# Symmetric score blocks with DMA-transposed mirrors, and rows scattered by expert, in an attention plus mixture-of-experts kernel

## The chip, the cores and the metric

One core of a Trainium2 chip runs the whole program in one launch. The metric is device time in microseconds (us), the median of three runs. The engines are PE (TensorE matmuls), PEld (TensorE weight loads, which may lie beside matmuls), DVE (VectorE), ACT (ScalarE), POOL (GpSimd) and SP (SyncE, which here only issues transfers). Transfers run on 16 DMA engines, whoever issues them.

## The reference

```python
# attention: u, v are (8, 2816, 256), z is (8, 2816, 64)
scores = (1/2816) * matmul(z, z.transpose(0, 2, 1))   # (8, 2816, 2816)
attn = maximum(scores, 0) ** 2
x = (u * matmul(attn, v)).reshape(22528, 256)
# mixture of experts: 8 experts, hidden size 512
y_dense = maximum(x @ w1_dense, 0) @ w2_dense
logits = x @ w_gate                                   # (22528, 8)
e = argmax(logits);  gate = softmax(logits)[e]
y_moe = gate * (maximum(x @ w1[e], 0) @ w2[e])        # each row uses one expert only
out = y_dense + y_moe
```

Two facts of this arithmetic matter later: `scores` is the product of `z` with itself, so each batch's matrix is symmetric, and each row of `x` needs only the expert that its largest logit names.

## The kernel before

Rows are cut into blocks of 128; a batch has 22 of them. Inputs are float32, matmul operands are cast to bfloat16.

**Attention stage.** For each of 8 batches, `zT` (64 x 2816) is made by 22 TensorE transposes (L59) with a DVE cast each (L61), and `v` is cast by DVE (L68). Six groups of up to four query blocks (512 columns, the last group 256) each run over all 22 key blocks. For a key block, `do_sc` makes a score tile of 128 x 512 (L81), ACT applies relu and the scale (L89), DVE squares it (L90), and two matmuls add its product with `vtile` to `outT` (L100). All 22 x 22 score blocks are computed. `outT` has the features on partitions, so it is copied out, transposed back on TensorE (L113), multiplied by `u` (L121), and written to `x_bridge` in DRAM (L122).

**Weight stage.** All expert weights are loaded in float32 and cast once (L131 to L145).

**Expert stage.** 44 tiles of 512 rows. A tile loads `x_bridge` (L156), transposes it on TensorE, computes logits, and makes a gate row for each expert with two reductions on POOL (L170, L175). The function `ffn` runs for the dense layer and then for every one of the 8 experts, on an input that was multiplied by the gate row of that expert (L208), which is zero for rows that belong elsewhere. All add into `yT`. The result is transposed back and written (L219 to L222). All transfers are issued by SP. A tile scheduler sets the order on each engine.

## Time and profile before

| what | value |
|---|---|
| median of three runs | 2951.72 us (2950.89 to 2952.02) |
| span of the profiled execution, first to last instruction | 2948.5 us |
| mean granted TensorE clock | 0.981 of full speed |
| busy: PE, DVE, ACT, POOL | 2665.0, 1825.7, 1473.0, 221.3 us |
| attention, weight and expert stage in that span | 0 to 1004, 1004 to 1053, 1053 to 2949 us |

The profiled execution has no time of its own beside the span; the median of the runs is 3.2 us longer than the span, and that is taken as what lies around it. Busy time of PE counts each matmul from its start to its end, and neighbours overlap, so 90% of the span is not 90% of what PE can do; the distance from one start to the next tells that. The shares are averages over two long stages with different limits, so the stages are read apart.

### The profile page before, as it was taken

What the parts mean: (1) busy time and instruction counts of PE and PEld (TensorE: products, weight loads), DVE (VectorE), ACT (ScalarE), POOL (GpSimd) and SP (SyncE); (2) the same over time, 40 slices, a digit from 0 to 9 for tenths busy, and PEclk for the clock granted to TensorE, in tenths of its full rate; (3) what the DMA queues carried; (4) which work ended last, traced back from release to release, by engine and by line L of the source; (5) the groups of instructions that cost most, each with busy time, mean ns of one, the idle gap of its engine ahead of it and who ended that gap; (6) DMA issues with size and microseconds to landing.
All of it is one profiled execution on the core that took longest, in us unless ns stands there. A gap on an engine that the chain in (4) does not pass through costs nothing.

```text
span 2948.5 us, 34413 instructions
## 1 busy us (share of the span) xinstructions
PE 2665.0 (90%) x11176; PEld 1020.7 (35%) x11176; DVE 1825.7 (62%) x3586; ACT 1473.0 (50%) x2685; POOL 221.3 (8%) x94
## 2 busy tenths in 40 slices
PE   7999999999999569999999999989899998999997
PEld 2323233232332123333333333333333333333333
DVE  7889888888889645445445544544555455455543
ACT  4556656566566324444444444444444444444443
POOL 0000000000000011011101110110111011101100
PEclk9999999999999879999999999999999999999999
DMA  6231221311111400000000000000000000000000
GB/s 177 88 94 54 93 87 56 94 55 54 40 54 50 159 20 27 30 23 23 28 28 22 24 29 26 22 26 29 24 22 28 29 21 26 27 26 23 26 26 15
DMA packets 165381, 133.18 MB, mean 45 GB/s; under 512 B 45648, under 2 KB 162896, under 8 KB 165200
## 3 DMA queue, kind: packets, MB, share of 16 engines
q1 hardware_dynamic: 165200, 130.99, 14.6%
q8 instruction: 87, 1.43, 0.2%
q14 instruction: 94, 0.77, 0.1%
HBM read 84.42 MB, written 46.14 MB: 44 GB/s over the span
## 4 chain that ended last, share of the span: by engine, by line
PE 60%; DVE 12%; ACT 10%; issue 7%; POOL 7%; DMA 2%; ACTq 0%; DVEq 0%; POOLq 0%; SPq 0%
PE yT L194 19%; PE outT L100 13%; PE h_ps L190 12%; PE sc_ps L81 9%; ACT hs L192 6%; POOL se L175 5%; DVE attn_sb L90 3%; PE scps L204 3%; DVE xTe L208 3%; ACT attn_f L89 3%; POOL mx L170 3%; DVE gw L177 2%; PE tp L113 2%; PE yp L219 2%; PE xp L158 1%
## 5 line engine op out<-in xcount | busy, mean ns | idle before, releaser
L192 ACT ACTIVATE hs<-h_ps 128x512 bf16<-128x512 f32 x1584 | 863.0, 593 | 992.0 <-PE h_ps L190 989.8
L194 PE MATMUL yT<-hs,w2e 128*128 128x512 bf16 x2816 | 796.5, 379 | 117.0 <-ACT hs L192 113.4
L190 PE MATMUL h_ps<-xTe,w1e 128*128 128x512 bf16 x2816 | 800.8, 379 | 0.4 <-DVE xTe L208 0.4
L89 ACT ACTIVATE attn_f<-sc_ps 128x512 f32<-128x512 f32 (+1 forms) x1056 | 585.2, 561 | 411.8 <-DVE attn_sb L90 234.8
L208 DVE TENSOR_TENSOR xTe<-xT,scps 128x512 bf16<-128x512 bf16 x704 | 451.6, 676 | 404.0 <-PE h_ps L190 400.1
L90 DVE TENSOR_TENSOR attn_sb<-attn_f 128x512 bf16<-128x512 f32 (+1 forms) x1056 | 649.2, 639 | 29.0 <-ACT attn_f L89 21.6
L100 PE MATMUL outT<-attn_sb,vtile 128*128 128x512 bf16 (+1 forms) x2112 | 586.1, 370 | 19.0 <-DVE attn_sb L90 13.4
L194 PEld LDWEIGHTS <-w2e 128*128 128x128 bf16 x2816 | 277.4, 101 | 480.9 <-issue 293.5
L190 PEld LDWEIGHTS <-w1e 128*128 128x128 bf16 x2816 | 275.0, 98 | 327.7 <-issue 2.2
L81 PE MATMUL sc_ps<-zT 64*128 64x512 bf16 (+1 forms) x1056 | 367.5, 371 | 17.1 <-ACT attn_f L89 1.8
L170 POOL PARTITION_ALL_REDUCE mx<-lg x44 | 78.4, 1783 | 2582.4 <-DVE lg L167 2582.4
L160 DVE CAST xT<-xp 128x128 bf16<-128x128 f32 x352 | 101.3, 288 | 262.1 <-PE xp L158 261.9
L100 PEld LDWEIGHTS <-vtile 128*128 128x128 bf16 x2112 | 167.6, 103 | 237.3 <-issue 185.2
L177 DVE RECIPROCAL gw<-se 8x512 f32<-8x512 f32 x44 | 147.0, 3342 | 98.6 <-POOL se L175 98.6
L81 PEld LDWEIGHTS <-zT 64*128 64x128 bf16 x1056 | 91.5, 93 | 308.3 <-issue 286.2
L204 PE MATMUL scps<-sca,ones 1*128 1x512 bf16 x352 | 135.2, 384 | 46.1 <-DVE xTe L208 46.1
L221 DVE COPY yo<-yp 128x128 f32<-128x128 f32 x352 | 101.5, 288 | 111.2 <-PE yp L219 65.7
L158 PE MATMUL xp<-ident,xs 128*128 128x128 f32 x352 | 107.6, 306 | 49.8 <-DMA xs<-x_bridge 43.8
L175 POOL PARTITION_ALL_REDUCE se<-ex x44 | 142.2, 3233 | 64.6 <-ACT ex L173 64.6
L117 DVE COPY xt<-tp 128x128 f32<-128x128 f32 x352 | 101.4, 288 | 57.0 <-PE tp L113 54.5
L113 PE MATMUL tp<-ident,oS 128*128 128x128 f32 x352 | 113.3, 322 | 3.9 <-DVE xt L117 1.2
L194 PE MATMUL yT<-hs,w2d 128*128 128x512 bf16 x352 | 109.8, 380 | 4.8 <-ACT hs L192 0.7
(35 smaller groups left out, 985.7 us busy)
## 6 DMA issues: line engine op xcount, KB each, us to landing
vtf<-in_v_dram SPq DMA_DIRECT2D x8, 2816.0 KB, 10.9
ut<-in_u_dram SPq DMA_DIRECT2D x176, 128.0 KB, 2.1
x_bridge<-xt SPq DMA_DIRECT2D x176, 128.0 KB, 1.7
xs<-x_bridge SPq DMA_DIRECT2D x176, 128.0 KB, 2.1
out_dram<-yo SPq DMA_DIRECT2D x176, 128.0 KB, 1.7
c<-in_moe_w_dram SPq DMA_DIRECT2D x2, 4096.0 KB, 20.4
zTf<-in_z_dram SPq DMA_DIRECT2D x8, 704.0 KB, 5.1
sca<-sca_all SPq DMA_DIRECT2D x352, 1.0 KB, 1.6
```

The source lines that it names most:

```text
L81: nc.tensor.matmul(out=sc_ps[k][:], lhsT=zT[:, k * P:(k + 1) * P], rhs=zT[:, i0 * P:i0 * P + W], start=True, stop=True,)
L89: nc.scalar.activation(attn_f[:], sc_ps[k][:], AF.Relu, scale=scale)
L90: nc.vector.tensor_mul(attn_sb[k][:], attn_f[:], attn_f[:])
L100: nc.tensor.matmul(out=outT[d][:], lhsT=vtile[:, k, d * P:(d + 1) * P], rhs=a[:], start=(k == 0), stop=(k == nK - 1),)
L113: nc.tensor.transpose(out=tp[:], in_=oS[d][:, j * P:(j + 1) * P], identity=ident[:],)
L175: nc.gpsimd.partition_all_reduce(se[:], ex[:], E, bass_isa.ReduceOp.add)
L177: nc.vector.reciprocal(gw[:], se[:])
L190: nc.tensor.matmul(out=h_ps[:], lhsT=w1t(fc, d), rhs=xin[d][:], start=(d == 0), stop=(d == 1))
L192: nc.scalar.activation(hs[:], h_ps[:], AF.Relu)
L194: nc.tensor.matmul(out=yT[d][:], lhsT=w2t(fc, d), rhs=hs[:], start=(first and fc == 0), stop=(last and fc == 3))
L204: nc.tensor.matmul(out=scps[:], lhsT=ones1[:], rhs=sca0[:], start=True, stop=True)
L208: nc.vector.tensor_mul(xTe[d][:], xT[d][:], scps[:])
```

## The change

**Attention.** In each batch, `score_chunk` makes only the blocks on and above the diagonal, 253 of 484, in strips: strip `k` holds key block `k` against blocks `k` to 21, in chunks of up to 8 blocks (1024 columns). `end_strip` has SP issue one DMA transpose for a strip, which fills tile `T` with the mirrored blocks. `av` makes one 128-row output block of 256 columns from 22 matmuls; its stationary operand is a block of a strip `A` where `k <= i`, else a block of `T`, so the result already has rows on partitions and no TensorE transpose is left. `zT` and the transposed `x` come from DMA transposes as well (L78, L204). `z` is loaded twice, side by side, so that the contraction is over 128 and the scale is halved. Scores run ahead of `av` by `LEAD` = 9 steps, with 4 buffers for `T`.

**Routing.** Every 11 blocks, `route_a` and `route_b` turn logits into a gate, an expert and a running position within that expert. `scatter` has POOL issue an indirect DMA that writes 128 rows of 576 bytes (x in bfloat16, gate, row number) to their places in DRAM array `xs`. Weights are cast by POOL-issued DRAM-to-DRAM transfers into `wb`.

**Expert stage.** A table made by 32 DVE instructions gives each of 95 tiles of 256 rows (88 and 7 for ragged ends) its start row and its one expert. `fetch` reads both into registers on SP, transposes the rows by DMA, and loads that expert's weights (512 KB) and the gates. A tile runs the dense layer and that one expert; `finish` scales, adds and has POOL scatter the rows to `out`, two indirect DMAs a tile.

The attention core of the new file:

```diff
+        zT = zpool.tile([P, nK, P], BF, name="zT")
+        nc.sync.dma_start_transpose(
+            out=zT[:], in_=zn[:].rearrange("p k h d -> p (k h d)"))
...
+            k0, k1 = h * nK // 2, (h + 1) * nK // 2
+            nc.gpsimd.dma_start(out=vb[:, k0:k1, :], in_=src[:, k0:k1, :])
...
+        def score_chunk(b, k, c0, c1):
+            zT = zT_of[b]
+            w = c1 - c0
+            s_ps = psS.tile([P, 8, P], F32, name="s_ps")
+            for h in range(0, w, 4):
+                hw = min(4, w - h)
+                nc.tensor.matmul(out=s_ps[:, h:h + hw, :], lhsT=zT[:, k, :],
+                                 rhs=zT[:, k + c0 + h:k + c0 + h + hw, :],
+                                 start=True, stop=True)
+            r = aw.tile([P, 8, P], F32, name="r")
+            nc.scalar.activation(r[:, :w, :], s_ps[:, :w, :], AF.Relu, scale=0.5 / S)
+            nc.vector.tensor_mul(A[b, k][:, c0:c1, :], r[:, :w, :], r[:, :w, :])
...
+        def end_strip(b, k):
+            n = nK - 1 - k
+            if n:
+                T[b, k] = aT.tile([P, nK - 1, P], BF, name="T")
+                nc.sync.dma_start_transpose(
+                    out=T[b, k][:, :n, :],
+                    in_=A[b, k][:, 1:, :].rearrange("p n c -> p (n c)"))
...
+        def av(b, i):
+            o = psV.tile([P, D], F32, name="o")
+            vb = v_of[b]
+            for k in range(nK):
+                lhsT = A[b, k][:, i - k, :] if k <= i else T[b, i][:, k - i - 1, :]
+                nc.tensor.matmul(out=o[:], lhsT=lhsT, rhs=vb[:, k, :],
+                                 start=(k == 0), stop=(k == nK - 1))
+            return o
...
+        def gate_x(g, o):
+            pay = pays[(g // G) % 3]
+            x = pay[:, g % G, 0:D]
+            nc.vector.tensor_mul(x, o[:], ut_of.pop(g))
+            xT = aw.tile([P, 2, P], BF, name="xT", bufs=6)
+            nc.sync.dma_start_transpose(out=xT[:], in_=x)
+            xT_of[g] = xT
...
+        def scatter(g):
+            q, j = divmod(g, G)
+            ins = nc.gpsimd.indirect_dma_start(
+                out=xs, out_offset=bass.IndirectOffsetOnAxis(ap=rs[q][:, j:j + 1], axis=0),
+                in_=pays[q % 3][:, j, :].bitcast(F32), in_offset=None)
+            nodep("xs", ins)
...
+        LEAD = 9
+        rate = (nK + 1) / 2
+        for g in range(nB + 8):
+            if g < nB:
+                b, i = divmod(g, nK)
+                must = strip_end[b, min(i + 1, nK - 1)]
+                want = rate * (g + 1 + LEAD * min(1.0, (g + 1) / LEAD) - 1)
+                produce(max(must, want))
```

The expert stage of the new file:

```diff
+        def fetch(s):
+            R = nc.values_load(Rt[0:1, s:s + 1], engines=[ET.SP], min_val=0,
+                               max_val=XROWS - T2,
+                               skip_runtime_bounds_check_because="made by the table")
+            e = nc.values_load(Et[0:1, s:s + 1], engines=[ET.SP], min_val=0, max_val=E - 1,
+                               skip_runtime_bounds_check_because="made by the table")
+            xT = mx.tile([P, 2, T2], BF, name="xT2")
+            rows = xs[bass.ds(R, T2), :]
+            nc.sync.dma_start_transpose(out=xT[:], in_=rows.bitcast(BF)[:, 0:D])
+            we = mx.tile([P, 2 * F + 4 * D], BF, name="we")
+            nc.sync.dma_start(out=we[:], in_=wb[bass.ds(e, 1), :, :].rearrange("o p f -> (o p) f"))
+            me = mx.tile([P, 2, 2], F32, name="me")
+            nc.sync.dma_start(out=me[:], in_=rows[:, P:P + 2]
+                              .rearrange("(j p) c -> p j c", p=P))
+            return xT, we, me
...
+        def up(xT, w1):
+            h_ps = psH.tile([P, 4, T2], F32, name="h_ps")
+            for f in range(4):
+                for c in range(2):
+                    nc.tensor.matmul(out=h_ps[:, f, :], lhsT=w1(c, f), rhs=xT[:, c, :],
+                                     start=(c == 0), stop=(c == 1))
+            h = mh.tile([P, 4, T2], BF, name="h")
+            nc.scalar.activation(h[:], h_ps[:], AF.Relu)
+            return h
...
+        def down(h, w2, name):
+            y = psY.tile([P, 2, D], F32, name=name)
+            for j in range(2):
+                for f in range(4):
+                    nc.tensor.matmul(out=y[:, j, :], lhsT=h[:, f, j * P:(j + 1) * P],
+                                     rhs=w2(f), start=(f == 0), stop=(f == 3))
+            return y
...
+            for j in range(2):
+                nc.vector.tensor_scalar(out=ys[:, j, :], in0=ye[:, j, :], scalar1=me[:, j, 0:1],
+                                        scalar2=None, op0=ALU.mult)
+            nc.vector.tensor_add(ys[:], ys[:], yd[:])
+            for j in range(2):
+                ins = nc.gpsimd.indirect_dma_start(
+                    out=out, out_offset=bass.IndirectOffsetOnAxis(ap=ix[:, j:j + 1], axis=0),
+                    in_=ys[:, j, :], in_offset=None, bounds_check=N - 1, oob_is_err=False)
...
+        AHEAD = 3
+        got = {s: fetch(s) for s in range(AHEAD)}
+        pend = None
+        for s in range(NT + 1):
+            if s < NT:
+                xT, we, me = got.pop(s)
+                hd = up(xT, lambda c, f: w1d[:, c, f * P:(f + 1) * P])
+            if pend is not None:
+                ps_, he_, yd_, we_, me_ = pend
+                ye_ = down(he_, lambda f: we_[:, 2 * F + f * D:2 * F + (f + 1) * D], "ye")
+                finish(ps_, yd_, ye_, me_)
+            if s < NT:
+                if s + AHEAD < NT:
+                    got[s + AHEAD] = fetch(s + AHEAD)
+                he = up(xT, lambda c, f: we[:, c * F + f * P:c * F + (f + 1) * P])
+                yd = down(hd, lambda f: w2d[:, f, :], "yd")
+                pend = (s, he, yd, we, me)
```

**What stands in a row on PE in the attention stage.** Before, in the middle of a group, a score matmul of 512 columns stands between pairs of output matmuls of 512 columns (`sc_ps` the score tile, `outT` the output with features on partitions):

```order
L81 LDWEIGHTS zT
L81 MATMUL sc_ps<-zT 128x512 [waits Activation_49]
L100 LDWEIGHTS vtile
L100 MATMUL outT_4749<-attn_sb,vtile 128x512 [waits DVE_49]
L100 LDWEIGHTS vtile
L100 MATMUL outT_4750<-attn_sb,vtile 128x512
L81 LDWEIGHTS zT
L81 MATMUL sc_ps<-zT 128x512 [waits Activation_49]
```

After, in the middle of a batch, a score chunk comes first and then the 22 output matmuls of a step, 256 columns each, each with its own weights (`A` a strip, `T` a mirrored strip; the first five of the 22 are shown):

```order
L142 MATMUL s_ps<-zT 128x512 [waits Activation_49]
L142 LDWEIGHTS zT
L142 MATMUL s_ps<-zT 128x512
L188 LDWEIGHTS A_4010
L188 MATMUL o<-vb,A_4010 128x256 [waits DVE_49]
L188 LDWEIGHTS A_4077
L188 MATMUL o<-vb,A_4077 128x256
L188 LDWEIGHTS A_4160
L188 MATMUL o<-vb,A_4160 128x256
L188 LDWEIGHTS A_4243
L188 MATMUL o<-vb,A_4243 128x256
L188 LDWEIGHTS T [waits DMAHW2_49]
```

Each output matmul before waited for DVE's square of its own score tile; now the step waits once for DVE to have emptied its output buffer, and at the first block of `T` for a DMA transpose.

**What stands in SP's queue in the attention stage.** Before, plain loads of `u` and `v` and stores of `x`:

```order
L122 DMA x_bridge<-xt 128x256 [waits DVE_49]
L122 DMA x_bridge<-xt 128x256 [waits DMAHW1_49,DVE_49]
L120 DMA ut<-in_u_dram 128x256 [waits DMAHW2_49]
L122 DMA x_bridge<-xt 128x256 [waits DMAHW3_49,DVE_49]
L120 DMA ut<-in_u_dram 128x256 [waits DMAHW4_49]
L120 DMA ut<-in_u_dram 128x256 [waits DMAHW6_49,DMAHW5_49]
L122 DMA x_bridge<-xt 128x256 [waits DVE_49]
```

After, at the end of the second batch's strips, DMA transposes only: `T` is a mirrored strip out of `A14` to `A20`, `xT` the transposed x of one block out of a payload tile:

```order
L204 DMA_TRANSPOSE xT_1799<-pay0_70 128x2x128 [waits DVE_49]
L153 DMA_TRANSPOSE T_1810<-A16_1803 128x5x128 [waits DMAHW2_49,DMAHW3_49,DVE_49,PE_49]
L153 DMA_TRANSPOSE T_1819<-A17_1812 128x4x128 [waits DMAHW5_49,DVE_49,PE_49]
L204 DMA_TRANSPOSE xT_1847<-pay0_70 128x2x128 [waits DMAHW4_49,DVE_49]
L153 DMA_TRANSPOSE T_1857<-A18_1851 128x3x128 [waits DMAHW6_49,DVE_49,PE_49]
L153 DMA_TRANSPOSE T_1865<-A19_1859 128x2x128 [waits DMAHW0_49,DVE_49,PE_49]
L153 DMA_TRANSPOSE T_1873<-A20_1867 128x1x128 [waits DMAHW2_49,DMAHW7_49,DVE_49,PE_49]
L204 DMA_TRANSPOSE xT_1905<-pay0_70 128x2x128 [waits DVE_49]
L204 DMA_TRANSPOSE xT_1963<-pay0_70 128x2x128 [waits DMAHW1_49,DVE_49]
L153 DMA_TRANSPOSE T_1989<-A0_1924 128x21x128 [waits DMAHW3_49,DVE_49,PE_49]
```

The loads moved to POOL's queue. Each `T` waits for PE (a buffer four strips back), and an `xT` that stands behind it waits with it.

**What stands in SP's queue in the expert stage.** Before, a gate row for each expert (`sca`), loads of x and stores of the output:

```order
L156 DMA xs_17762<-x_bridge 128x256 [waits DMAHW7_49,PE_49]
L203 DMA sca0_16926<-sca_all_16641 1x16x32 [waits DMAHW6_49,DMAHW2_49,PE_49]
L203 DMA sca0_17060<-sca_all_17027 1x16x32 [waits DMAHW4_49,DVE_49,PE_49]
L203 DMA sca0_17096<-sca_all_17027 1x16x32 [waits DMAHW6_49,DMAHW0_49,PE_49]
L203 DMA sca0_17132<-sca_all_17027 1x16x32 [waits DMAHW7_49,DMAHW1_49,PE_49]
L156 DMA xs_17376<-x_bridge 128x256 [waits PE_49]
L203 DMA sca0_17168<-sca_all_17027 1x16x32 [waits DMAHW3_49,DMAHW0_49,PE_49]
```

After, one tile's `fetch`: two register loads (TENSOR_LOAD), a DMA transpose, the weights and the gates; the stores moved to POOL:

```order
L418 TENSOR_LOAD Rt_8486
L421 TENSOR_LOAD Et_8487
L425 ISA
L425 DMA_TRANSPOSE xT2_8680<-xs 128x2x256 [waits DMAHW4_49,PE_49]
L427 ISA
L427 DMA we_8682<-wb 128x2048 [waits DMAHW5_49,PE_49]
L429 ISA
L429 DMA me_8684<-xs 128x2x2 [waits DMAHW6_49,DVE_49]
```

Each of the three transfers waits for the buffer of four tiles back, and all that follows on SP waits behind it.

## Rows read from the trace of the kernel before

**Rows 1.** The page: span, then busy time of each engine over the span.

```profile
span 2948.5 us, 34413 instructions
...
PE 2665.0 (90%) x11176; PEld 1020.7 (35%) x11176; DVE 1825.7 (62%) x3586; ACT 1473.0 (50%) x2685; POOL 221.3 (8%) x94
...
q1 hardware_dynamic: 165200, 130.99, 14.6%
```

**Rows 2.** Three windows, one for each stage: length, then busy time (instructions) per engine.

```profile
core 0: us, PE busy (x) PEld busy (x) DVE busy (x) ACT busy (x) POOL busy (x), PEclk, DMA share, GB/s
0.00:1004.00 1004.00, 950.52 (x3696) 300.65 (x3696) 881.09 (x1865) 586.44 (x1057) 0.68 (x6) 0.98 0.25 76
1004.00:1053.00 49.00, 7.56 (x17) 2.52 (x18) 13.53 (x15) 1.09 (x2) 1.10 (x1) 0.50 0.60 201
1053.00:2949.00 1896.00, 1706.94 (x7464) 717.49 (x7462) 931.13 (x1706) 885.50 (x1626) 219.56 (x88) 0.99 0.08 25
```

**Rows 3.** Attention, one key block in the timeline: start, length, instruction, idle before.

```profile
151.76 0.67 DVE L90 TENSOR_TENSOR attn_sb<-attn_f 128x512 bf16<-128x512 f32 x1
...
151.77 0.61 PE L100 MATMUL outT<-attn_sb,vtile 128*128 128x512 bf16 x2
...
152.42 0.39 PE L81 MATMUL sc_ps<-zT 64*128 64x512 bf16 x1
152.52 0.28 DVE L61 CAST zT<-ztp 64x128 bf16<-64x128 f32 x1
152.53 0.60 ACT L89 ACTIVATE attn_f<-sc_ps 128x512 f32<-128x512 f32 x1 [0.37 <-PE ztp L59]
152.73 0.67 DVE L90 TENSOR_TENSOR attn_sb<-attn_f 128x512 bf16<-128x512 f32 x1
```

**Rows 4.** TensorE alone in the timeline, 256-column and 512-column matmuls back to back.

```profile
139.61 0.61 PE L100 MATMUL outT<-attn_sb,vtile 128*128 128x256 bf16 x4
...
140.90 0.28 PE L100 MATMUL outT<-attn_sb,vtile 128*128 128x256 bf16 x1
...
1103.78 1.03 PE L190 MATMUL h_ps<-xTe,w1e 128*128 128x512 bf16 x4
```

**Rows 5.** Groups by line and shape: count, busy us, mean ns, idle before.

```profile
L90 DVE TENSOR_TENSOR attn_sb<-attn_f 128x512 bf16<-128x512 f32 x880 | 580.1, 683 | 25.1 <-ACT attn_f L89 21.1 <-PE outT L100 2.3
...
L89 ACT ACTIVATE attn_f<-sc_ps 128x512 f32<-128x512 f32 x880 | 520.2, 597 | 362.1 <-DVE attn_sb L90 216.2 <-PE sc_ps L81 99.1 <-PE ztp L59 27.4
...
L175 POOL PARTITION_ALL_REDUCE se<-ex x44 | 142.2, 3233 | 64.6 <-ACT ex L173 64.6
...
L90 DVE TENSOR_TENSOR attn_sb<-attn_f 128x256 bf16<-128x256 f32 x176 | 69.8, 419 | 3.8 <-ACT attn_f L89 0.5
L89 ACT ACTIVATE attn_f<-sc_ps 128x256 f32<-128x256 f32 x176 | 65.3, 383 | 49.7 <-PE tp L113 20.8 <-DVE attn_sb L90 18.6 <-PE sc_ps L81 9.8
```

**Rows 6.** Waits of the whole run: who waited for whom, us, times, longest.

```profile
PE yT L194 <- ACT hs L192: 114.1, 313, 1.0
...
DVE gw L177 <- POOL se L175: 98.6, 44, 3.0
```

**Rows 7.** DMA issues: transfer, times, KB each, median us from issue to landing.

```profile
vtf<-in_v_dram SPq DMA_DIRECT2D x8, 2816.0 KB, 10.9
ut<-in_u_dram SPq DMA_DIRECT2D x176, 128.0 KB, 2.1
...
zTf<-in_z_dram SPq DMA_DIRECT2D x8, 704.0 KB, 5.1
sca<-sca_all SPq DMA_DIRECT2D x352, 1.0 KB, 1.6
...
a<-in_moe_w_gate_dram SPq DMA_DIRECT2D x1, 8.0 KB, 1.7
```

**Rows 8.** SyncE's queue at L54 and L203: ns min/median/max of one DMA issue.

```profile
L54 SPq DMA_DIRECT2D zTf<-in_z_dram x8: 368/378/434, 0.7 to 651.1; - x8
...
L203 SPq DMA_DIRECT2D sca<-sca_all x352: 497/502/1266, 1062.9 to 2913.9; - x176
```

**Rows 9.** The weight stage in two windows: lengths and busy times, granted clock, DMA share, GB/s.

```profile
1004.00:1031.00 27.00, 0.00 (x0) 0.00 (x0) 6.03 (x5) 0.00 (x0) 0.00 (x0) 0.50 0.99 335
1031.00:1053.00 22.00, 7.56 (x17) 2.52 (x18) 7.50 (x11) 1.09 (x2) 1.10 (x1) 0.50 0.12 36
```

More of the change, by code (lines that the diff above doesn't have):

```diff
@@ L6 @@
 from concourse._compat import with_exitstack
-from concourse.masks import make_identity
 F32 = mybir.dt.float32
+I32 = mybir.dt.int32
 BF = mybir.dt.bfloat16
 AF = mybir.ActivationFunctionType
+ALU = mybir.AluOpType
+AX = mybir.AxisListType
+ET = mybir.EngineType
 P = 128
@@ new lines @@
+    G = 11
+    assert nK % G == 0
+    T2 = 256
+    NT = N // T2 + E - 1
+    ROW = 288
+    CAP = N
+    XROWS = E * CAP
+    xs = nc.dram_tensor("xs", (XROWS, ROW // 2), F32, kind="Internal")[:]
+    wb = nc.dram_tensor("wb", (E, P, 2 * F + 4 * D), BF, kind="Internal")[:]
+    uf = u.rearrange("b (n p) d -> p (b n) d", p=P)
+    ctx.enter_context(tc.manual_schedule(engines={ET.PE, ET.Activation, ET.DVE, ET.SP}))
+    const = ctx.enter_context(tc.tile_pool(name="const", bufs=1))
+    wg = const.tile([P, 2, E], BF, name="wg")
@@ new lines @@
+    w1d = const.tile([P, 2, F], BF, name="w1d")
+    w2d = const.tile([P, 4, D], BF, name="w2d")
+    ones = const.tile([P, P], BF, name="ones")
+    ntri = const.tile([P, P], BF, name="ntri")
+    smask = const.tile([P, E, G], F32, name="smask")
+    desc8 = const.tile([P, G, E], F32, name="desc8")
+    tok = const.tile([P, nB], I32, name="tok")
+    base = const.tile([P, E], F32, name="base")
+    ecap = const.tile([P, E], F32, name="ecap")
+    pays = [const.tile([P, G, ROW], BF, name=f"pay{i}") for i in range(3)]
@@ new lines @@
+    zT_of, v_of = {}, {}
+    zT_of[0] = load_z(0)
+    v_of[0] = load_v(0)
+    nc.vector.memset(ones[:], 1.0)
+    nc.vector.memset(smask[:], 1.0)
+    nc.vector.memset(smask[:, :, 0], 0.0)
+    for p_ in pays:
+        nc.vector.memset(p_[:], 0.0)
+    for e in range(E):
+        for h in range(T2 // P):
+            r0 = e * CAP + h * P
+            nc.gpsimd.dma_start(out=xs[r0:r0 + P, :], in_=pays[2][:, 0, :].bitcast(F32))
+    nc.vector.memset(ntri[:], -1.0)
+    nc.gpsimd.affine_select(out=ntri[:], in_=ntri[:], compare_op=ALU.is_ge,
+                            fill=0.0, base=0, pattern=[[-1, P]],
+                            channel_multiplier=1)
@@ new lines, with produce @@
+                n = nK - k
+                nch = -(-n // 8)
+                edges = [round(n * j / nch) for j in range(nch + 1)]
+                for j in range(nch):
+                    total += edges[j + 1] - edges[j]
+                    work.append((total, b, k, edges[j], edges[j + 1], j == 0, j == nch - 1))
+                strip_end[b, k] = total
+        wi = [0]
+        def produce(upto):
+            while wi[0] < len(work):
+                tot, b, k, c0, c1, first, last = work[wi[0]]
+                if tot - (c1 - c0) >= upto:
+                    break
+                if first:
+                    new_strip(b, k)
+                score_chunk(b, k, c0, c1)
+                if last:
+                    end_strip(b, k)
+                wi[0] += 1
@@ new lines, in av, with load_u @@
+        def av(b, i):
[6 more added lines that the diff above has]
+            return o
+        ut_of, xT_of, lg_of, rs = {}, {}, {}, {}
+        def load_u(g):
+            ut = aw.tile([P, 2, D], F32, name="ut", bufs=4)
+            nc.gpsimd.dma_start(out=ut[:], in_=uf[:, g:g + 2, :])
+            ut_of[g], ut_of[g + 1] = ut[:, 0, :], ut[:, 1, :]
@@ new lines, in gate_x, with logits @@
+        def gate_x(g, o):
[5 more added lines that the diff above has]
+            xT_of[g] = xT
+        def logits(g):
+            q, j = divmod(g, G)
+            if j == 0:
+                lg_of[q] = psL.tile([P, G, E], F32, name="lg")
+            xT = xT_of.pop(g)
+            for c in range(2):
+                nc.tensor.matmul(out=lg_of[q][:, j, :], lhsT=xT[:, c, :],
+                                 rhs=wg[:, c, :], start=(c == 0), stop=(c == 1))
@@ new lines, in weights, with at @@
+        def weights(e):
+            nc.gpsimd.dma_start(
+                out=wb[e, :, 0:2 * F].rearrange("p (c f) -> p c f", c=2),
+                in_=moe_w1[e].rearrange("(c p) f -> p c f", p=P))
+            nc.gpsimd.dma_start(
+                out=wb[e, :, 2 * F:].rearrange("p (c d) -> p c d", c=4),
+                in_=moe_w2[e].rearrange("(c p) d -> p c d", p=P))
+        later = {}
+        def at(step, fn):
+            later.setdefault(step, []).append(fn)
+        load_u(0)
+        load_u(2)
```

374 lines of the change are left out of this document (199 added, 175 removed).

## The prediction

> **What bounds the kernel now.** I read the page first: the span is 2948.5 us and PE looks 90% busy [rows 1]. That share mixes two stages, so the windows come next: attention takes 1004 us, the weights 49 us, the experts 1896 us [rows 2]. Then each stage is read in its own timeline.
>
> In attention the limit is DVE. One key block starts 0.97 us after the one before it (151.76 to 152.73), and DVE fills that with the square, 0.67 us, and a cast of 0.28 us [rows 3]; over the stage it is busy for 881 of 1004 us [rows 2]. PE needs only three matmuls of 512 columns in that time. Back to back such a matmul costs (1.03 - 0.39)/3 = 0.213 us, and one of 256 columns (0.61 - 0.28)/3 = 0.11 us, each with weights of its own, so the weight load is hidden at both widths [rows 3, 4].
>
> In the expert stage the limit is PE's own work: 1896/44 = 43.1 us a tile, of which 154 matmuls of 512 columns (2 for logits, 8 for broadcasts, 9 x 16 for the layers) take 154 x 0.213 = 32.8 us. The other 10 us are 16 transposes and waits such as that for ACT (114 us in all 44 tiles), and the gate chain that POOL's reduction starts is short in what it makes others wait (98.6 us) [rows 6].
>
> **The change part by part.** The sum is made against the span, 2948.5 us; the median of the runs is 3 us above it, and 3 us are added at the end.
>
> *PE in attention.* Scores: 8 x 253 blocks of 128 columns are 259,000 columns, at 0.213 us for 512 about 108 us. Output: 8 x 22 x 22 = 3872 matmuls of 256 columns at 0.11 us are 426 us. 352 tiny logit matmuls are taken at half of a 256-column one: 19 us. Together 553 us, where the stage before had 1004 us. This is the floor of the new stage.
>
> *ACT and DVE in attention.* From widths 256 and 512, ACT costs 0.169 us and 0.836 ns a column, DVE 0.155 us and 1.03 ns a column [rows 5]. 336 chunks of 770 columns on average give ACT 273 us and DVE 319 us; with 176 gatings at 0.42 us and 16 rounds of routing of some 16 small instructions (88 elements, 0.25 us each by the same line, 64 us) DVE stays under 460 us. Both are below PE. The stage's old limit is gone.
>
> *DMA in attention.* This is what is late next. Blocks of 128 x 128 (32 KB) to be transposed: 8 x 231 off the diagonal, 2 x 176 for x, 176 for z, 2376 in all. No trace row shows a DMA transpose, so its price is bounded. Below: it must read rows of 256 bytes, as the load of z did: 704 KB, 22 blocks, landed in 5.1 us where a transfer of 1 KB took 1.6 us, so 3.5/22 = 0.16 us a block [rows 7]. Above: it writes a 16-row piece as 32 bytes into each of 128 partitions, so if each 32 bytes cost as much as one small piece, a block has 1024/16 = 64 pieces per DMA engine. The 8 KB load in 256 pieces of 32 bytes took 1.7 us against 1.6 us for 16 pieces, so 0.1/15 = 7 ns a piece [rows 7] and 0.45 us a block. I take 0.20 us, nearer to the load of z, whose reads are the same. That is 2376 x 0.20 = 475 us, with ends of 380 and 1070 us. Other traffic on the same 16 engines: v 8 x 10.9 = 87 us; u, as many bytes, 87 us; z twice, 16 x 3.5 = 56 us; scattered rows, 13 MB at the rate of z, 63 us; 8.4 MB of weights at 335 GB/s, 25 us [rows 7, 9]. Sum 318 us. DMA in attention is thus 475 + 318 = 793 us against PE's 553: the stage becomes bound by transfers. Its ends are 700 and 1390 us.
>
> *SP's queue.* 352 transposes at the 0.37 to 0.50 us of an issue [rows 8] are at most 176 us; DMA's 793 us hide them, and without that cover they would come one after another with the transfers' 1.6 us of latency [rows 7]. Each T also waits for a buffer four strips back. Near the end of a batch the xT queued behind it comes late, and PE's logits, which stand ahead of the next step's outputs, wait for that xT: about one landing and two blocks, some 3 us, in each of 8 batches. While DMA is the bound that lies inside the 793 us.
>
> *Start and turn.* z must land, be transposed, pass ACT and DVE and be transposed again before the first output: 5.1 + 6 + 3 + 6 us and a little, 25 us. Between the stages: a transpose, routing, 11 scatters at about 1 us, their landing, a fetch: 30 us. The table lies beside the scatters. The old weight stage with its 49 us goes; its half clock, 0.50 while PE was idle [rows 9], can show in this gap as well.
>
> *Expert stage.* A tile has 32 matmuls of 256 columns: 3.52 us on PE. ACT: two of 1024 columns at 1.03 us, 2.1 us; DVE two of 256 and one of 512, 1.5 us [rows 5]. DMA: 4 blocks of transpose 0.8 us, 512 KB of weights at 335 GB/s 1.6 us, 256 KB out at the same 0.8 us, gates 0.1 us: 3.3 us [rows 9]. SP: three issues, 1.5 us, and two register loads that no row prices. POOL: two indirect DMAs; no POOL transfer is in this trace (all bytes went by SP's queue [rows 1]), so one is bounded by SP's 0.43 us [rows 8] and by 3.23 us, POOL's longest instruction [rows 5]: 0.9 to 6.5 us a tile. Four resources stand within a few tenths of each other and fetches run only three tiles ahead, so I take a fifth above PE: 4.2 us, 95 x 4.2 = 400 us; ends 334 and 614 us. Removed are 1896 us.
>
> Sum: 25 + 793 + 30 + 400 + 8 (last tile out) + 3 = 1259 us.
>
> **The rivals.** *A: PE stays the bound of attention.* If a block costs 0.10 us or less, DMA is at most 238 + 318 = 556 us and hides behind PE: with expert tiles at 3.9 us the whole is 25 + 553 + 30 + 370 + 11 = 989 us, and with stalls up to 1120. For it speaks that windows with plain loads ran at 335 GB/s [rows 9], which is 0.10 us for 32 KB; against it, that the same bytes in 256-byte rows took 0.16 us [rows 7]. The Trainium skill, Advanced Engine Details and Errata, section X-Bar Transpose (TRN2), says that transposing DMAs are as fast as regular ones and expects 350 to 400 GB/s; by that rule this rival holds. No run here shows it yet.
>
> *B: pieces or POOL set the pace.* At 0.45 us a block attention takes 1390 us and the whole 1856 us. Or POOL needs 3.23 us for an indirect DMA: then the expert stage takes 614 us, and the whole 1473 us; POOL's 331 transfers in attention would take 1069 us at that price, and the whole, with both, 25 + 1069 + 30 + 614 + 11 = 1749 us. When PE waits so much, the clock may fall to the half that the weight stage shows [rows 9], which would double PE's 3.52 us as well. The Trainium skill, DMA: Bandwidth & Descriptors, section SWDGE vs HWDGE vs iDMA, says that software on GpSimd writes the descriptors of POOL-issued transfers, one pair for each piece; no run here prices it.
>
> *C: slower than before.* The transpose moves single elements of 2 bytes, not rows. A block is 16,384 elements, 1024 per engine, at 7 ns 7.2 us a block: attention 17 ms. The point from which this decides is (2949 - 466 - 318)/2376 = 0.91 us a block, twice my upper bound. Nothing in the trace excludes it, since no transpose is there.
>
> **How the numbers follow.** The forecast (1120 to 1400 us) gets 0.45, A 0.23, B 0.28 (a sixth of it above 1850 us), C 0.04. The predicted time is the sum, rounded to 1250 us. The range must reach into A and B: 985 to 1850 us, which leaves out some 0.15. The forecast's own range is 1120 to 1400 us. Runs of this kernel agree within 0.04%, so 0.2% either way is what a measurement tells from no change; for that only a corner of B and C is left: faster 0.95, same 0.01, slower 0.04.
>
> **What would show it right or wrong.** In the new trace: attention near 790 us with DMA busy near all the time and PE's first T block waiting for a DMA transpose; PE starting a 256-column matmul every 0.11 us inside a step; ACT and DVE each idle over a third; an expert tile every 4.2 us. A step of 3.2 us with no wait for T says A. A block price above 0.3 us, POOL's queue always behind, or a clock of half speed says B. The prediction is wrong if the transposes cost outside 0.10 to 0.45 us a block, if scatters stall the payload buffers, or if the two register loads on SP, which no row prices, make a tile longer than 5 us.

## The result and the profile after

The changed kernel takes 1301.9 us (median of five runs, 1292.6 to 1322.1) where the kernel before took 2951.4 us beside it: a ratio of 0.441 (0.438 to 0.443). The forecast was 1250 us, with 1120 to 1400 us as its own range. Medians here and below are of all runs of a kernel, ratios of those within 1.5% of its fastest. The profiled execution has a span of 1320.4 us and a time of 1322.1 us, the longest of the five, so its rows run some 20 us above the median.

The page after: span, busy time per engine, busy tenths in 40 slices (PE, granted clock, DMA), DMA queues.

```profile
span 1320.4 us, 21386 instructions
...
PE 989.1 (75%) x7905; PEld 776.5 (59%) x7928; DVE 607.9 (46%) x1190; ACT 456.3 (35%) x543; POOL 510.5 (39%) x532
...
PE   1425867777687767577787677887199899999996
...
PEclk9867987889887888797899889888599999999998
DMA  9999879969959997995995995983299999999894
...
q1 hardware_dynamic: 406592, 140.38, 59.6%
q0 software_dynamic: 97872, 82.36, 37.5%
```

Against [rows 1]: PE's busy time fell from 2665 to 989 us, and the packets of the transfer queues, one at 14.6% before, together come to 97% of the 16 engines' span. The row of DMA tenths is what to read first. It stands at 9 through nearly all of the expert stage and most of attention, falls to 5, 6 or 7 some once in each batch of attention, and to 3 and 2 only in the turn between the stages, where the row of PE falls to 1.

Windows of the changed kernel: up to the first score, three pieces of attention's start, the rest of attention, the turn, the expert stage. The last three columns are granted clock, DMA share, GB/s. A share above 1 means that more packets were under way than there are engines, each counted in full; so a high share says how much was under way, and not that the engines could do no more.

```profile
core 0: us, PE busy (x) PEld busy (x) DVE busy (x) ACT busy (x) POOL busy (x), PEclk, DMA share, GB/s
0.00:22.80 22.80, 0.00 (x0) 0.00 (x0) 4.81 (x8) 1.28 (x1) 12.10 (x22) 1.00 1.35 159
22.80:134.00 111.20, 50.39 (x270) 31.15 (x272) 32.81 (x40) 24.59 (x30) 32.51 (x42) 0.79 1.43 155
134.00:235.00 101.00, 75.95 (x585) 57.46 (x587) 50.34 (x92) 30.94 (x42) 34.81 (x36) 0.86 0.89 152
235.00:345.00 110.00, 81.08 (x623) 60.33 (x625) 56.33 (x100) 34.15 (x47) 38.01 (x38) 0.89 1.07 153
345.00:930.00 585.00, 437.70 (x3394) 331.20 (x3408) 290.54 (x530) 171.64 (x235) 193.41 (x196) 0.87 0.92 144
930.00:953.00 23.00, 0.30 (x2) 0.10 (x1) 17.14 (x44) 0.00 (x0) 12.71 (x11) 0.51 0.15 42
953.00:1316.00 363.00, 343.64 (x3040) 296.23 (x3040) 155.92 (x380) 193.68 (x190) 186.90 (x190) 0.97 0.96 237
```

Against [rows 2], attention went from 1004 to about 925 us, the weight stage with its 49 us became a turn of some 28 us, and the expert stage went from 1896 to 363 us. Nearly all of the gain is in the experts; attention, on which the argument was spent, became 8% shorter. Lengths times shares give the DMA time up to 930 us: 31 + 159 + 90 + 118 + 538 = 936 us.

The chain of waits, largest first, of the changed kernel: who waited for whom, us, times, longest.

```profile
ACT r L146 <- PE s_ps L142: 412.8, 124, 21.7
POOL ut L196 <- DVE pay L202: 333.0, 43, 18.8
...
PE lg L213 <- DMA xT<-pay: 137.2, 44, 8.7
...
PE o L188 <- DMA T<-A: 89.1, 17, 17.6
```

ACT and POOL are idle for want of work and cost nothing. What costs is in the last two rows: PE stands 226 us for two kinds of DMA transpose.

The start, PE alone in the timeline (a bracket is the idle time before, and its releaser):

```profile
22.84 1.78 PE L142 MATMUL s_ps<-zT 128*128 128x512 bf16 x4 [22.84 <-DMA zT<-zn]
...
28.49 0.42 PE L188 MATMUL o<-vb,A 128*128 128x256 bf16 x1
40.26 4.66 PE L188 MATMUL o<-vb,T 128*128 128x256 bf16 x21 [11.36 <-DMA T<-A]
...
63.61 3.74 PE L188 MATMUL o<-vb,T 128*128 128x256 bf16 x19 [8.39 <-DMA T<-A]
```

The first output starts at 28.5 us, but its second matmul already needs `T` and waits until 40.3 us, while everything else that was issued at the start is under way as well (share 1.43). In the first 134 us such waits take 56 us.

SP's queue and PE in one stretch of attention:

```profile
158.81 7.25 SPq L153 DMA_TRANSPOSE T<-A  x3
...
166.11 2.52 SPq L204 DMA_TRANSPOSE xT<-pay  x2
...
168.91 0.20 PE L213 MATMUL lg<-wg,xT 128*128 128x8 bf16 x2 [4.02 <-DMA xT<-pay]
```

Three `T` stand in 7.25 us of SP's queue. The row joins them: by the trace's records each holds SP for 1.1 to 1.3 us, and in the rest SP waits until the next may go. The `xT` behind them goes out at 166.1 us, and PE, whose logits stand ahead of the next outputs, waits 4.0 us for it. The transfers are far from full just then, with a DMA share of 0.28 and 0.33:

```profile
154.00:164.00 10.00, 9.95 (x91) 8.19 (x91) 8.21 (x23) 4.64 (x6) 2.01 (x2) 1.00 0.28 64
164.00:174.00 10.00, 5.98 (x40) 4.05 (x38) 4.20 (x6) 1.73 (x2) 7.87 (x9) 0.83 0.33 94
```

Two tiles of the expert stage on PE:

```profile
1202.43 1.04 PE L437 MATMUL h_ps<-xT,w1d 128*128 128x256 bf16 x8
1203.30 1.04 PE L447 MATMUL ye<-we,h 128*128 128x256 bf16 x8
1204.18 1.04 PE L437 MATMUL h_ps<-xT,we 128*128 128x256 bf16 x8
1205.05 1.04 PE L447 MATMUL yd<-w2d,h 128*128 128x256 bf16 x8
1205.92 1.04 PE L437 MATMUL h_ps<-xT,w1d 128*128 128x256 bf16 x8
```

Eight matmuls of 256 columns take 0.87 us from start to start, 0.109 us each, as in [rows 4]; a tile without a wait takes 3.49 us (1202.43 to 1205.92), against 363/95 = 3.82 us on average in this execution.

### The profile page after: what moved, and what is told of

The parts are those of the page before. It is cut to its first block, busy times and chain, and to the rows that moved or that the text cites. A ratio compares the mean times of both kernels' runs of the same rounds, so it can differ in the third digit from the quotient of the medians.

```text
span 1320.4 us, 21386 instructions
## 1 busy us (share of the span) xinstructions
PE 989.1 (75%) x7905; PEld 776.5 (59%) x7928; DVE 607.9 (46%) x1190; ACT 456.3 (35%) x543; POOL 510.5 (39%) x532
## 3 DMA queue, kind: packets, MB, share of 16 engines
q8 instruction: 62, 1.02, 0.4%
## 4 chain that ended last, share of the span: by engine, by line
DMA 26%; PE 26%; issue 22%; POOL 11%; DVE 7%; another core or an unknown queue 3%; SPq 2%; ACT 2%; POOLq 0%; ACTq 0%; DVEq 0%
PE o L188 20%; DMA xT<-pay 13%; DMA T<-A 11%; POOL out_dram L461 10%; PE s_ps L142 5%; DVE A L147 4%; ACT r L146 2%; SPq L153 2%; DVE pay L202 1%; DMA vb<-in_v_dram 1%; POOL xs L270 1%; PE lg L213 1%; SPq L78 1%; POOL xs L103 0%
## 5 line engine op out<-in xcount | busy, mean ns | idle before, releaser
L146 ACT ACTIVATE r<-s_ps 128x768 f32<-128x768 f32 (+3 forms) x336 | 258.2, 811 | 588.2 <-PE s_ps L142 412.8
L147 DVE TENSOR_TENSOR A<-r 128x768 bf16<-128x768 f32 (+3 forms) x336 | 308.7, 957 | 233.6 <-ACT r L146 193.8
L188 PE MATMUL o<-vb,T 128*128 128x256 bf16 x1848 | 263.7, 298 | 91.2 <-DMA T<-A 89.1
L188 PE MATMUL o<-vb,A 128*128 128x256 bf16 x2024 | 281.2, 294 | 4.7 <-DVE pay L202 2.9
L188 PEld LDWEIGHTS <-T 128*128 128x128 bf16 x1848 | 195.8, 107 | 135.6 <-DMA T<-A 94.9
L440 ACT ACTIVATE h<-h_ps 128x1024 bf16<-128x1024 f32 x190 | 193.7, 1023 | 186.5 <-PE h_ps L437 137.7
L461 POOL DMA_INDIRECT out_dram<-ys,ix x190 | 186.9, 984 | 179.2 <-DVE ys L459 142.0
L188 PEld LDWEIGHTS <-A 128*128 128x128 bf16 x2024 | 212.0, 106 | 72.8 <-issue 18.9
L270 POOL DMA_INDIRECT xs<-pay,posi x176 | 194.0, 1102 | 117.5 <-DVE posi L265 68.7
L142 PE MATMUL s_ps<-zT 128*128 128x512 bf16 (+3 forms) x609 | 159.9, 373 | 38.7 <-DMA zT<-zn 22.8
```

The lines of the kernel that those rows point to most:

```text
L142: nc.tensor.matmul(out=s_ps[:, h:h + hw, :], lhsT=zT[:, k, :], rhs=zT[:, k + c0 + h:k + c0 + h + hw, :], start=True, stop=True)
L146: nc.scalar.activation(r[:, :w, :], s_ps[:, :w, :], AF.Relu, scale=0.5 / S)
L147: nc.vector.tensor_mul(A[b, k][:, c0:c1, :], r[:, :w, :], r[:, :w, :])
L188: nc.tensor.matmul(out=o[:], lhsT=lhsT, rhs=vb[:, k, :], start=(k == 0), stop=(k == nK - 1))
L270: ins = nc.gpsimd.indirect_dma_start(out=xs, out_offset=bass.IndirectOffsetOnAxis(ap=rs[q][:, j:j + 1], axis=0), in_=pays[q % 3][:, j, :]. ...
L440: nc.scalar.activation(h[:], h_ps[:], AF.Relu)
```

## The experiments

All runs stood beside runs of the kernel before, which took 2950 to 2951 us in every group. e1 to e4 ran in one group, e5 to e8 in a second, e9 with e10, and e11 with e12; the runs of the changed kernel stand apart from all of these.

Differences inside a group can be trusted further than differences between groups: one and the same kernel took 1180 us in one group and 1260 us in another (e8 and e11, below). The changed kernel's profiled execution bears the mark of the slower groups. Its expert stage takes 357 us from the first matmul to the last, and the same code takes 336 to 342 us in e1 to e8 and 350 and 353 us in e11 and e9; by the trace's records the weight loads of that stage pause for over 1.5 us five times, and never in e1 to e8. So what is compared with the changed kernel's 1301.9 us, itself of another group, can be off by some tens of microseconds.

**e1: no mirror transposes; e2: more of them.** e1 leaves out the transposes of the strips and reads the mirrored blocks as they are, so its output blocks mix wrong factors. e2 transposes up to 9 blocks of each strip a second time into a tile that nobody reads, 1224 blocks more.

```diff
 # e1
+            return
...
-                lhsT = A[b, k][:, i - k, :] if k <= i else T[b, i][:, k - i - 1, :]
+                lhsT = A[b, k][:, i - k, :] if k <= i else A[b, i][:, k - i, :]
 # e2, in end_strip
+                nc.sync.dma_start_transpose(
+                    out=T2_[:, :min(n, 9), :],
+                    in_=A[b, k][:, 1:1 + min(n, 9), :].rearrange("p n c -> p (n c)"))
```

> The DMA transposes of the strips are left out (168 of them, 1848 blocks of 32 KB); where the kernel reads a mirrored block it reads the block on the other side of the diagonal untransposed, so that part of the output matmul is not what the reference asks. Theory 1, attention is bound by the throughput of the 16 DMA engines: some 1848 x 0.22 = 400 us of transfers go, what is left is about 530 us, less than PE's 553 us, so attention falls from about 925 to about 600 us and the whole from 1302 to about 980 us. Theory 2, attention is bound by order in SP's queue (PE's logits wait for a transposed x that stands behind a strip waiting for its buffer): the same waits go too, so it also falls to about 1000 us; this run bounds what the mirrors cost in all. Theory 3, PE itself or its clock is the bound: at most 100 us go, about 1200 us.

> Each strip transpose is followed by a second one of its first 9 blocks at most (1224 more blocks in all) into a scratch tile that nobody reads; the output is the reference's. Theory 1, throughput of the DMA engines: 1224 x 0.22 = 270 us more, about 1570 us, unless the idle share of DMA takes some of it (then about 1500 us). Theory 2, order and latency in SP's queue: 168 more issues and landings, 0 to 1.5 us each where they lie before an x that is waited for, so 1302 to about 1450 us. Theory 3, PE or clock: no change, about 1300 us.

e1 took 995.4 us (987.0 to 1000.5), e2 1506.3 us (1504.3 to 1520.8). Between the two lie 1848 + 1224 blocks, so a block costs 511/3072 = 0.166 us. The changed kernel, of another group, lies on that line: 995 + 1848 x 0.166 = 1302 us.

Two limits of this price have to be known. e1 ends where PE is the bound, so what it takes off is the least that its 1848 blocks cost. And both edits change 168 transposes in SP's queue together with the blocks, so they don't part the engines' throughput from SP's queue: by the trace's records SP's transposes hold that queue for 749 us of the changed kernel's first 927 us, and for 979 of 1126 us in e2. That the queue follows the transfers, more than it sets their pace, is argued from two things: e4, below, has as many transposes and fewer packets of POOL's, and its hold falls to 694 us; and while PE waits for `T` in the changed kernel, 25 packets are under way on average for 16 engines.

The two windows of e1, attention with the turn, and experts:

```profile
22.50:642.00 619.50, 557.08 (x4890) 449.49 (x4891) 445.16 (x802) 261.01 (x352) 313.70 (x321) 0.97 0.77 119
642.00:990.00 348.00, 336.21 (x3040) 298.19 (x3038) 156.73 (x380) 194.38 (x190) 186.92 (x190) 0.98 1.01 247
```

Without the mirrors PE is busy 557 of 620 us, a share of 0.77 is left on DMA, and the clock stays at 0.97 where the changed kernel had 0.79 to 0.89. This is rival A's stage (PE at its floor of 553 us), and it exists only because the transposes are gone. In e2 PE's wait for `xT` grows to 324 us:

```profile
PE lg L218 <- DMA xT<-pay: 324.0, 96, 13.3
PE o L193 <- DMA T<-A: 81.5, 20, 12.3
```

**e3: logits later.** The logits of a block run 7 steps behind it, not 3, and `xT` has 9 buffers, not 6, so the `xT` may come late.

```diff
-            xT = aw.tile([P, 2, P], BF, name="xT", bufs=6)
+            xT = aw.tile([P, 2, P], BF, name="xT", bufs=9)
...
-            if 0 <= g - 3 < nB:
-                logits(g - 3)
+            if 0 <= g - 7 < nB:
+                logits(g - 7)
```

> The logits of a block are computed 7 steps after its output instead of 3 (9 buffers for the transposed x instead of 6), so PE has four more steps before it needs an x that stands behind strips in SP's queue. Theory 1, throughput of the DMA engines: PE waits as long for the mirrored strips instead; 1280 to 1302 us. Theory 2, order in SP's queue: PE's 137 us of waits for the transposed x go, about 1180 us.

It took 1238.5 us (1234.0 to 1253.4), a ratio of 0.4215 (0.4188 to 0.4242): 63 us less than the changed kernel of the other group, of which part may be the groups' difference (the two profiled executions differ by 18 us in the expert stage, whose code is the same). PE's waits in e3:

```profile
PE o L188 <- DMA T<-A: 200.8, 46, 17.6
...
PE lg L213 <- DMA xT<-pay: 2.6, 3, 1.1
```

The wait for `xT` is gone, and 112 of its 137 us come back as a wait for `T`; the same bytes move. So order in SP's queue does cost time, but less than its waits add up to: both theories hold in part.

**e4: z loaded once.** The second copy of `z` is made by DVE on the chip.

```diff
-        for h in range(2):
-            nc.gpsimd.dma_start(out=zn[:, :, h, :], in_=src)
+        nc.gpsimd.dma_start(out=zn[:, :, 0, :], in_=src)
...
+        nc.vector.tensor_copy(zn[:, :, 1, :], zn[:, :, 0, :])
```

> z is loaded once from DRAM and its second copy is made by VectorE (8 copies of 128 x 1408), where the kernel loads it twice. Theory 1, throughput of the DMA engines: half of z's packets go, 22,528 at about 41 ns over 16 engines, 58 us, about 1245 us. Theory 2, order in SP's queue: the transposes of z come three steps later and nothing else changes, 1290 to 1310 us.

Three runs took 1238 to 1270 us, and the fourth 1905 us, which nothing here explains. So the gain is 30 to 60 us and no closer, and this too is against the other group. By the trace's packet records, the packets that write `z` (128 bytes each) took 116 us of all 16 engines in the changed kernel and 50 us here.

**e5: weights later.** Two tiny transfers from a late payload hold each batch's cast of an expert's weights back from the start of the batch.

```diff
+            late = pays[(g // G) % 3][0:1, g % G, 0:D]
+            for c in (0, 2 * F):
+                nc.gpsimd.dma_start(out=wb[e, 0:1, c:c + D], in_=late)
```

> The loads and casts of the expert weights (16 transfers on GpSimd's queue, which the scheduler placed together into the first 70 us) are each held back until a block of x of the batch in which they are called is ready, by two tiny writes into the same place. Theory 1, throughput of the DMA engines over the whole stage: the bytes are the same, only moved, 1280 to 1302 us. Theory 4, the start is crowded: PE waited some 60 us for mirrored strips in the first 134 us, beside these transfers; 20 to 50 us go, about 1260 us.

1281.0 us (1268.0 to 1290.6). That is 21 us below the changed kernel's median, of another group of runs; with e11 in view, below, this is not settled.

**e6: e3, e4 and e5 together.**

> Logits 7 steps later, z loaded once, and weights later, all three. The first gave 63 us, the second 38 us. Theory 1, throughput of the DMA engines, with order in SP's queue as a part of it: the two add, some 100 us, and weights later gives 0 to 30 us; 1170 to 1200 us. If the gains are of one and the same wait, about 1230 us.

1222.4 us (1209.8 to 1253.5), 59 us below e5 in the same group. This is the one gain of logits later and z once that is measured inside a group. The gains don't add to the 100 us expected: PE still waits 199.0 us for `T`.

**e7: all blocks computed.** No mirror, no `T`: all 484 score blocks of a batch are made again, for four query blocks at a time, with the output still in its natural layout and `z` loaded once.

```diff
+            t = aA.tile([P, nK * GS, P], BF, name="Ag", tag="Ag", bufs=4)
...
-                lhsT = A[b, k][:, i - k, :] if k <= i else T[b, i][:, k - i - 1, :]
+                lhsT = A[b, i // GS][:, k * min(GS, nK - i // GS * GS) + i % GS, :]
```

> No mirrors and no symmetry: all 484 score blocks of a batch are computed in groups of 4 query blocks, no strip is transposed; z is loaded once. Transfers fall to about 470 us of DMA time; PE gets 98 us more (651 us), ScalarE 488 chunks of up to 1024 columns at 1.02 us (498 us), VectorE the same at 1.2 us plus 134 us (720 us). Theory 1, the DMA engines were the bound: VectorE bounds attention now, 720 to 760 us with the start, about 1150 us in all, faster than with mirrors. If the mirrors cost less than the blocks that they save: 1302 us or more.

1189.2 us (1183.6 to 1193.5), 33 us below e6 in the same group (24 us by the ratios, 0.403 against 0.411), though PE makes nearly twice the scores. The costliest group is now DVE's square (1212 ns on average, 1220 ns for the 480 of 1024 columns), and DVE is busy for 856 us:

```profile
L151 DVE TENSOR_TENSOR Ag<-r 128x1024 bf16<-128x1024 f32 (+1 forms) x488 | 564.7, 1212 | 94.4 <-ACT r L150 94.0
```

**e8: the square made cheaper.** ACT writes its relu in bfloat16, ACT squares one chunk in five, and logits run 7 steps behind.

```diff
-            r = aw.tile([P, 8, P], F32, name="r")
+            r = aw.tile([P, 8, P], BF, name="r")
...
-            nc.vector.tensor_mul(dst, r[:, :w, :], r[:, :w, :])
+            nch[0] += 1
+            if nch[0] % 5 == 0:
+                nc.scalar.activation(dst, r[:, :w, :], AF.Square)
+            else:
+                nc.vector.tensor_mul(dst, r[:, :w, :], r[:, :w, :])
```

> As the kernel that computes all blocks, with VectorE relieved: the relu result is bfloat16 in place of float32, one square in five is made by ScalarE, and logits come 7 steps later. ScalarE 498 + 98 x 1.02 = 598 us, VectorE at most 390 x 1.2 + 134 = 602 us, PE 651 us. Theory 1: PE bounds attention at about 660 to 690 us, about 1070 us in all. If PE was slowed by something else than transfers, no better than with all squares on VectorE.

1179.8 us (1177.9 to 1180.3), 9 us less than e7 and 110 us above the 1070 us expected. DVE's instruction of 1024 columns fell from 1220 to 693 ns, and the time hardly moved: the wait is elsewhere. One step in the timeline of e8:

```profile
404.68 1.02 PE L144 MATMUL s_ps<-zT 128*128 128x512 bf16 x4
406.44 0.59 PE L144 MATMUL s_ps<-zT 128*128 128x512 bf16 x2 [0.74 <-ACT r L150]
406.87 2.56 PE L189 MATMUL o<-vb,Ag 128*128 128x256 bf16 x22
```

The three chunks of a step stand one behind the other on PE, and the third waits for ACT to empty a score buffer (104 us over the run).

**e9: score chunks woven between the outputs.** e8, with one chunk put in after output matmuls 5, 11 and 17.

```diff
+                if k in (5, 11, 17) and wi[0] < len(work):
+                    produce(min(upto, work[wi[0]][0]))
...
-                produce(max(must, want))
+                produce(must if g else max(must, want))
```

> As the kernel that computes all blocks with VectorE relieved, but the up to three score chunks of a step stand between the output matmuls (before the 6th, 12th and 18th of 22) and not in one burst ahead of them, where the third waits 0.7 us for ScalarE to free one of two score buffers. If PE's order costs what its idle time shows, some 0.8 us of each 4.64 us step go: 176 x 0.8 = 140 us, about 1045 us. If ScalarE's work is the bound (598 us), the same: it is below PE's 651 us. If another wait takes its place, 1150 to 1180 us.

1158.4 us (1148.9 to 1161.9), a ratio of 0.392 (0.390 to 0.394): the shortest of all, and still 113 us above the 1045 us expected. The weaving does what it should where nothing else happens, and PE's wait for ACT falls to 54 us, from 104 us in e8 and 145 us in e10, which ran beside e9:

```profile
303.77 0.59 PE L144 MATMUL s_ps<-zT 128*128 128x512 bf16 x2
304.21 0.82 PE L192 MATMUL o<-vb,Ag 128*128 128x256 bf16 x6
```

**e10: expert weights loaded once.** e8, but only the first tile loads an expert's weights, and all tiles use those.

```diff
+            if s == 0:
+                we = mx.tile([P, 2 * F + 4 * D], BF, name="we", bufs=1)
+                nc.sync.dma_start(out=we[:], in_=wb[bass.ds(e, 1), :, :].rearrange("o p f -> (o p) f"))
...
+            we = we_all[0]
```

> As the kernel that computes all blocks with VectorE relieved, but the expert stage loads one expert's weights once and uses them for all 95 tiles, so the expert part of the output is not the reference's for most rows. The expert stage then moves 48 MB less. Theory PE: a tile of 3.8 us is 32 matmuls at 0.11 us and small waits, transfers are hidden; 1170 to 1180 us, no change. Theory transfers: the DMA engines, 0.96 busy in that stage, set the 3.8 us; a tile falls to 3.5 us, about 1150 us.

1269.3 us (1261.7 to 1270.7), 89 us more than e8, with 49 MB less to move. Most of it lies in attention, whose code is e8's: the first expert matmul comes at 904 us, where e8 has it at 830 us. The expert stage, from its first to its last matmul, took 356 us against 339 us. So both kernels ran once more, side by side.

**e11 and e12: e8 and e10 again.**

> The kernel of e8_all_blocks_split unchanged, beside e12 on one chip. If e10's longer attention stage (first expert matmul at 904 us against e8's 830 us) came from the chip of that run, this kernel is also slower here than its 1180 us, near 1250 us with a granted clock near 0.96. If it came from e10's edit, this kernel keeps 1175 to 1190 us.

> The kernel of e10_one_weight_load unchanged (only the first tile loads expert weights, all tiles use those). If the edit costs the attention stage 75 us, 1260 to 1275 us again while e11 stays at 1180 us. If the chip of that run did, this one lies within 15 us of e11, or below it: its expert stage moves 50 MB less.

e11, which is e8 unchanged, took 1259.5 us (1256.9 to 1262.6), and e12 1277.0 us (1256.9 to 1282.2), with ratios of 0.427 (0.426 to 0.428) and 0.429 (0.425 to 0.432). The edit of e10 therefore costs nothing measurable and gains nothing; something else made the groups of e9 to e12 slower than that of e8. The chip alone it was not: e8 and e10 stand on record with the same chip, e11 and e12 with another. Windows of e8 (first row) and of e11 (all others):

```profile
400.00:600.00 200.00, 173.93 (x1390) 128.12 (x1389) 101.53 (x213) 148.62 (x158) 68.76 (x72) 1.00 0.45 86
```

```profile
400.00:600.00 200.00, 161.41 (x1214) 118.14 (x1232) 89.72 (x183) 131.16 (x139) 61.02 (x66) 0.95 0.40 76
...
402.00:407.00 5.00, 4.84 (x27) 3.43 (x28) 2.08 (x3) 1.94 (x3) 3.86 (x4) 0.66 0.17 55
407.00:411.00 4.00, 0.80 (x4) 0.32 (x4) 0.56 (x2) 1.20 (x2) 1.73 (x2) 0.86 0.34 102
411.00:417.00 6.00, 6.00 (x28) 3.77 (x27) 1.62 (x3) 2.71 (x3) 0.00 (x0) 0.52 0.06 11
```

In e11, PE pauses for some microseconds (0.80 us busy in 407 to 411 us), and afterwards the granted clock is near its lower level, 1.2 GHz: 22 output matmuls take 4.90 us where they took 2.56 us in e8.

```profile
409.81 1.94 ACT L150 ACTIVATE r<-s_ps 128x1024 bf16<-128x1024 f32 x2 [5.86 <-remote]
...
410.88 1.01 PE L144 MATMUL s_ps<-zT 128*128 128x512 bf16 x2 [3.14 <-ACT r L150]
...
411.69 4.90 PE L189 MATMUL o<-vb,Ag 128*128 128x256 bf16 x22
```

Such places come near 252, 304, 360, 410, 520, 572 and 620 us, mostly some 52 us apart, which is the distance of 11 steps and so of a routing round; e12 shows them at the same times, and e8's granted clock stays at 1.00 until 780 us. What makes PE pause there in one group of runs and not in another stays open: 76 of PE's 8352 matmul records are missing in e11, PE's row names ACT, and ACT's names only `remote`, no instruction of this core. For this reason e9 is to be read against e10, which ran beside it with e8's attention: weaving is then worth some 110 us, 1158 against 1269, where e8 in its own group is 21 us away. That the pauses hit e9 and e10 alike is not shown.

e12's expert stage has a DMA share of 0.41 where e8's has 1.02:

```profile
880.00:1260.00 380.00, 333.10 (x2932) 284.13 (x2933) 164.02 (x401) 185.40 (x183) 189.46 (x191) 0.96 0.41 98
```

From the first to the last matmul that stage takes 371 us, and e11's beside it 350 us; in the other group e10's takes 356 us and e9's 353 us. With 49 MB less to move it is no shorter. So transfers don't set the pace of the expert stage, though their share is as high there as in attention: a high share by itself shows no bound.

## Why the prediction held, and where it was off

By its own terms, against the profiled execution: start 28.5 us (25 predicted), attention 897 us after that (793), turn 28 us (30), experts with the last tile 363 us (400 + 8), the rest about 5 us. Against this execution the sum is 5% low, by two errors of opposite sign: attention 104 us too short, experts 45 us too long. That it came so close is in part luck.

**What bounds attention: right in the main.** The stage is bound by its transfers (e1 and e7, without the mirrors, are shorter; SP's queue, which issues them, isn't parted from the engines that move them), PE waits for `T` and `xT` as foretold, and its own floor is where the prediction put it: with the mirrors gone (e1) PE is busy 557 us against 553.

**The price of a block: right within its bounds.** 0.166 us of time between e1 and e2, against 0.20 taken and 0.16 to 0.45 as ends; the row it was leaned on, the load of `z` in 256-byte rows [rows 7], gave 0.16. By the packet records the 2376 blocks took 524 us of the engines' time, 0.22 us each: a block is 128 packets of 256 bytes, whose median of 18 ns would make 0.14 us and whose mean was 27.6 ns. The rivals fall with it. A needed 0.10 us or less. By the Trainium skill, Advanced Engine Details and Errata, section X-Bar Transpose (TRN2), 350 to 400 GB/s would have made A true; 32 KB in 0.166 us are 197 GB/s, so for these strips, beside other traffic, the measurement differs from the page. B's pieces needed 0.45 us, C 0.91 us. The clock of B fell to 0.79 to 0.89 in attention, and not to half.

**The term that was mis-sized: "other traffic", 318 us.** The records give 936 - 524 = 412 us. Most of the difference is `z`, 116 us against 56 predicted: it was priced by a transfer without a cast, while POOL's casting transfer writes it in pieces of 128 bytes. `u` took 109 us against 87. The scattered rows were cheaper, 48 against 63.

**The step that failed: "While DMA is the bound that lies inside the 793 us".** SP's queue was read rightly (`T` ahead of `xT`, logits ahead of outputs), but the waits were put at 3 us in each batch and counted as hidden. They were 44 waits and 137 us. Letting the logits lag took them away and the time fell, by 63 us against the changed kernel (e3) and, together with z loaded once, by 59 us inside a group (e6 against e5). When the stage is bound by transfers, a wait of PE is free only if the DMA queues stay full meanwhile. Here the DMA share was 0.28 and 0.33 around one such wait, and SP's `T` stood for 222 us until PE came to a score matmul, so a late PE means a late transfer:

```profile
SPq L153 <- PE s_ps L142: 221.8, 98, 9.1
```

This chain is read from the rows; no run tests it by itself. The price of an issue was taken too low as well. SP's transposes, ns min/median/max:

```profile
L153 SPq DMA_TRANSPOSE T<-A x168: 1120/1702/10080, 28.9 to 903.7; - x168
```

```profile
L204 SPq DMA_TRANSPOSE xT<-pay x176: 1167/1220/3177, 45.4 to 926.1; - x176
```

against the 0.37 to 0.50 us of [rows 8] that the prediction used: with the 8 of `z`, 352 of them hold SP for 749 us, not 176, which is nearly as long as the transfers were to take.

**Start.** 25 us was right for the first output (28.5 us), but the next 100 us, in which `z`, `v`, `u` and the weights of the first batch compete with the first strips, were not seen as a place of their own: 56 us of waits for `T`.

**Expert tile: right in kind, too careful.** PE needs 3.49 us (3.52 predicted), and the whole came to 3.82 us, not 4.2; the same code in e1 to e8 takes 3.54 to 3.60 us (336 to 342 us for 95 tiles), so the fifth that was added to PE's time was hardly needed. POOL's indirect DMAs, bounded between 0.43 and 3.23 us, cost 0.98 us:

```profile
L461 POOL DMA_INDIRECT out_dram<-ys,ix x190 | 186.9, 984 | 179.2 <-DVE ys L459 142.0
```

so POOL needs 2 us of a tile, and B's POOL falls. The register loads did not make a tile longer than 5 us. PE alone sets the pace: removing 49 MB of loads made the stage no shorter (e10, e12).

**What the change could have done.** Mirrored blocks save PE 1848 x 128 columns of scores, 1848 x 128 x 0.213/512 = 98 us, and they cost 0.166 x 1848 = 307 us in transfers. The version that computes all blocks (e7) is 24 to 33 us shorter than the best version with mirrors in its own group (e6), and 113 us shorter than the changed kernel of the other group. The gain of the change as a whole is nearly all that of its expert stage. In attention it can't be that of the symmetry, since e7 does without; it may be the natural layout, which took DVE's casts and PE's transposes away, or the chunks of 1024 columns, and no run parts these.

## What to carry to other kernels

Before work is traded for transfers, price both on the engine that will be late next: here symmetry saved 98 us on an engine that had room and put 307 us on the one that had none. An engine that waits while transfers are the bound can still cost time when the next transfer hangs on its work, so read the order of each issuing queue together with the order of the engine that waits for it. And repeat a kernel that is to be compared beside the new one: a reference that keeps its time to 0.1% did not show that another kernel had moved by 7%. A share of transfers near 1 does not make them the bound: it stood there in attention, where taking transfers away gave 307 us, and in the expert stage, where it gave nothing.
